# Another order of the same steps in a one-core kernel of attention, token mixing and a gated MLP

## The chip, the cores and the metric

The kernel runs on one core of one Trainium2 chip. The metric is the device time of one execution in microseconds (us). Lower is better.

## The reference

Three blocks follow each other, all in float32, for 2 batches of 768 tokens and 512 channels (8 heads of 64).

- Attention: each query sees the keys less than 16 places away, and 24 summaries of blocks of 32 tokens (the maximum of the block's keys, the mean of its values). One softmax runs over both.
- Token mixing: `theta = x @ w_theta`; `zr = x*cos(theta)`, `zi = x*sin(theta)`; `y = w_tok_r @ zr + w_tok_i @ zi` over the tokens; `u = x + y`; `x = u + max(u @ w_ch, 0)`.
- Gated MLP: `h = gelu(x @ w_in)`, split into u and v of 512 channels; v is normalised over its channels and mixed over the tokens with `w_sg`, plus `b_sg`; the result is `x + (u * v_s) @ w_out`.

## The kernel before

**Steps and plan.** The kernel defines some 1,670 named steps (`op`, line 272). Each is a small function that issues one to a few dozen instructions on one engine. The string `PLAN` (lines 49 to 258) lists them in the order in which they are issued. An entry reads `name.engine.places~step`: the engine is P (TensorE), V (VectorE), A (ScalarE), G (GpSimd) or S (SyncE, which issues the loads and stores); the places are a page of SBUF memory in units of 64 bytes, a PSUM bank or the number of a small buffer; `~step` makes the instruction wait for that step on another engine as well. `Steps.play` (line 283) goes through the plan and calls the functions; the framework adds the waits that the data and the reuse of memory ask for. Every engine works through its own steps strictly in the plan's order, so a step that waits holds up all later steps of its engine. The plan is text made beforehand by a search, with a model of durations that is not part of the kernel.

**Names.** The attention works on pairs of heads p = 0 to 7 (0 to 3 are batch 0) and on two halves of the queries. `k0`, `q0_1`, `vT0`, `v0_1` are loads. `ks`, `vs` are the block summaries of keys (VectorE) and values (GpSimd or VectorE); `vp`, `vm`, `vr` bring the value summaries beside the values. `S0_1` is the scores, `m`, `d`, `e` maximum, subtraction and exponential, `PT` and `Pt` the transposition and its copy to SBUF, `O0_1_0` and `O0_1_1` the product with the values for each head, `n` the division, `X` the transposed result, `xe`, `xh`, `xl` its copy and its split.

Matmuls run as three matmuls each on a high part and a remainder of both factors (`mm3`, lines 383 to 388), so each factor is split first (`...h` the high part, `...l` the remainder). The weights come as 64-bit floats: `wth2d` loads a piece, `wth2t` (ScalarE, line 518) and `wth2r` (VectorE, line 525) make float32 of it, `wth2h` and `wth2l` split it.

`th1_3` is a theta step: tile 1 of 12 token tiles, channel group 3. It needs `xl3_0` and `wth3l`. `kk`, `rr`, `ab`, `sc` reduce theta to one turn and take sine and cosine, `zm`, `zh`, `zl` multiply by x and split. `y0_1_2_0` is a token-mixing step of batch 0: token tile 1, channel quarter 2, with `w_tok_r`; it needs `zl1_1` and the split weights `wr1`, `wri1`. `uv` adds x. `ch`, `iv`, `iu` and `o` are the products with w_ch, the two halves of w_in and w_out. They use seven products of half-size blocks in place of eight, with sums of blocks (`u0_0+2`, `wv1+0`) prepared on VectorE and GpSimd. `mn`, `st`, `sq`, `rv`, `vo` normalise v, `vn` splits it, `sg` mixes it over the tokens, `ga` and `gm` gate, `g` prepares the result for w_out.

**Before the scores** TensorE runs 97 small matmuls (`fill`), and `idle0`, `idle1` are 6 and 1 matmuls whose results are not used; their numbers stand in `IDLE`.

**The order of the first 40 us.** These are the plan's steps of three engines in their own order.

SyncE before, up to `wth3d`: `k1 q1_0 k2 vT1 q2_0 k0 q0_0 vT0 q0_1 vT2 q1_1 v0_0 q2_1 wth0d v2_0 q3_0 v1_0 v0_1 vT3 k3 wth1d q3_1 v2_1 v3_1 v1_1 v3_0 wth2d wr0d k4 wth3d`

TensorE before, from `PT2_0` on: `PT2_0 O0_0_0 O1_0_0 O1_0_1 O0_0_1 PT0_1 PT2_1 X0_0 PT1_1 X1_0 vp3 S3_1 S3_0 O0_1_0 O0_1_1 O2_0_0 O2_0_1 O1_1_0 O1_1_1 O2_1_0 PT3_1 th0_0 X2_0 th2_0 X0_1 PT3_0 O2_1_1 O3_1_0 O3_1_1 O3_0_0 O3_0_1 th1_0 X1_1 th1_1 th2_1 X3_0 th0_1 X3_1 th5_0 th1_2 th0_2 th2_2 X2_1 th1_3 th0_3`

ScalarE before, from `e3_1` on: `e3_1 vr3_0 e3_0 Pt3_1 wth3t wth2t Pt3_0 xe2_0 xe0_1 xh2_0 xh0_1 wth2h xe1_1 wr0t wth3h xe3_0 wi0t`

Of the kernel before, what the change touches and what calls it, by code (L numbers as in the profile page):

```python
# [49 lines left out]
ones.V masks.G band.G k1.S.1536 warm.V.2716 fill.P.7 identb.V maskb.A ks1.V.5 q1_0.S.312 S1_0.P.6  # L50
m1_0.V.0 k2.S.2128 ks2.V.6 sums.G d1_0.V.195 vT1.S.416 q2_0.S.608 idle0.P.0 S2_0.P.4 k0.S.1055
ks0.V.2 m2_0.V.1 q0_0.S.1463 sets.G idle1.P.0 S0_0.P.0 e1_0.A d2_0.V.2691 vs1.G.4 vT0.S.240 vs0.G.0
vp1.P.6 PT1_0.P.2 m0_0.V.4 d0_0.V.723 q0_1.S.1512 S0_1.P.4 m0_1.V.1 vp0.P.7 vm1.A.0 e2_0.A vT2.S.96
q1_1.S.72 v0_0.S.2447 Pt1_0.A.2544 q2_1.S.455 d0_1.V.626 S2_1.P.1 m2_1.V.0 vm0.A.1 wth0d.S.2176
d2_1.V.3 e0_0.A wth0t.A.1 vs2.G.2 v2_0.S.783 PT0_0.P.6 S1_1.P.4 Pt0_0.A.240 q3_0.S.288 vp2.P.7
v1_0.S.1743 PT2_0.P.0 vr0_0.G m1_1.V.1 e0_1.A vr1_0.G vm2.A.2 v0_1.S.1103 e2_1.A O0_0_0.P.3
O1_0_0.P.2 wth0r.V.687 d1_1.V.1403 O1_0_1.P O0_0_1.P Pt2_0.A.479 n0_0.V.4.1632 n1_0.V.1
wth0h.A.1920 vT3.S.720 k3.S.192 e1_1.A ks3.V.4 PT0_1.P.0 Pt0_1.A.240 PT2_1.P.6 X0_0.P.3 xe0_0.A
# [14 lines left out]
xh3_1.G.864~wr1r kk2.A.687 S4_1.P.3 rr1.V.2496 vs4.V.1 xl1_1.G~wr1r v4_1.S.479 m4_0.V.2 kk0.A.1248
k6.S.528 wr0h.A.1088 xl2_1.G~wr1r xl3_1.G~wr1r th4_0.P.5 th4_1.P d4_0.V.315 v4_0.S.719 vp4.P.1
th3_0.P.2 th3_1.P th5_1.P th3_2.P wri1t.A.0 th3_3.P q6_0.S.288 m4_1.V.0 wri1r.V.1186 th4_2.P
q7_1.S.360 wri0r.V.639 wri0h.G.1024~wri0r rr0.V.2464 d4_1.V.578 rr2.V.1568 e4_0.A k5.S.2128
ab1_0.A.1600 PT4_0.P.3 vm4.A.1 ks6.V.1 sc1_0.A th4_3.P wi0h.G.960~wri0r ab0_0.A.1888 kk3.A.415
vr4_0.G~wri0r S6_0.P.0 sc0_0.A Pt4_0.A.312 vT5.S.2640 e4_1.A vT6.S.2256 O4_0_0.P.4 O4_0_1.P
wi0l.G~wri0r th5_2.P rr3.V.1536 vs5.V.2 m6_0.V.4 PT4_1.P.2 vr4_1.A wr0l.G~wri0r wri0l.G~wri0r
Pt4_1.A.671 n4_0.V.0.2592 th5_3.P X4_0.P.4 O4_1_0.P.2 kk4.A.736 O4_1_1.P zm0_0.G wr1h.A.2048  # L80
ks5.V.3 d6_0.V.419 S5_0.P.0 zh0_0.G.832 wi1d.S.1792 zl0_0.G zm1_0.G y0_0_0_0.P.6.3 v6_0.S.1351
vs6.V.4 rr4.V.2544 wri1h.A.1984 m5_0.V.0 vp5.P.5 vm5.V.2 xe4_0.A y0_0_0_1.P d5_0.V.1299 wi1t.A.2
q5_1.S.1223 S6_1.P.4 y0_0_1_0.P.0 wri1l.G v5_0.S.591 vp6.P.1 ab2_0.A.1888 zh1_0.A.896 wi1r.V.496
k7.S.288 y0_0_1_1.P sc2_0.A m6_1.V.1 d6_1.V.1747 S5_1.P.4 vT7.S.1400 n4_1.V.1.672 zl1_0.G~wi1r
wr1l.G~wi1r wi1h.G.768~wi1r y0_1_0_0.P vr5_0.A wi1l.G~wi1r vm6.A.1 e5_0.A PT5_0.P.1 ks7.V.0
y0_1_0_1.P m5_1.V.5 wr2d.S.1472 v5_1.S.1167 kk5.A.2112 zm2_0.G~wi1r zh2_0.G.832 d5_1.V.1843 zl2_0.G
v6_1.S.2399 v7_0.S.1247 e6_0.A rr5.V.2176 S7_1.P.4 y0_1_1_0.P Pt5_0.A.1296 wr2t.A.1 e5_1.A
PT5_1.P.1 vs7.V.2 wri2t.A.2 m7_1.V.4 d7_1.V.1798 ab5_0.A.1600 y0_1_1_1.P PT6_0.P.4 vr6_0.A vr5_1.G
O5_0_0.P.7 O5_0_1.P Pt5_1.A.2256 O5_1_0.P.2 O5_1_1.P wr2r.V.544 ab1_1.V.2208 Pt6_0.A.336
wr2h.G.896~wr2r S7_0.P.4 wri2r.V.512 n5_0.V.1 wri2h.A.128 wi2d.S.1856 n5_1.V.5 O6_0_0.P.1 O6_0_1.P  # L90
# [1105 lines left out]
```

## Time and profile before

| | |
|---|---|
| median of 3 runs | 377.17 us (375.05, 377.17, 377.32) |
| the profiled execution | 374.89 us, span 373.0 us |
| busy | PE 360.2 us (97%), DVE 293.0 (79%), ACT 216.6 (58%), POOL 162.8 (44%) |
| read from HBM, written | 36.86 MB, 3.15 MB |
| chain that ended last | PE 86%, DMA 7%, SPq 2%, ACT 2%, POOL 1%, DVE 1% |

The profile calls TensorE PE, VectorE DVE, ScalarE ACT, GpSimd POOL and SyncE SP. The span runs from the first to the last instruction. A row of a timeline names the start, the length, the engine, the line of the kernel, what is written and read, and in brackets the idle time before it with what ended it. `page4F` is a page of SBUF memory that many buffers use in turn, `banks` is PSUM. Lengths of neighbouring rows overlap a little, since an engine starts the next instruction before the last one's results are written.

### The profile page before, as it was taken

How to read it: one execution, taken by the hardware profiler on the slowest of the kernel's cores; microseconds unless marked ns; L12 is line 12 of the kernel's file. 1: busy time of each engine (PE TensorE's matmuls, PEld its weight loads, DVE VectorE, ACT ScalarE, POOL GpSimd, SP SyncE). 2: the span in 40 equal slices, each digit the busy share in tenths (PEclk: the TensorE clock that was granted, in tenths of full speed). 3: DMA queues.
4: the chain of work that ended last, by engine and by line, in shares of the span. 5: the costliest groups of instructions: out<-in, count | busy, mean ns of one | idle time of the engine just before them, and what ended most of it. 6: DMA issues, size and time to landing. Idle time of an engine off the chain costs nothing.

```text
span 373.0 us, 8181 instructions
## 1 busy us (share of the span) xinstructions
PE 360.2 (97%) x3236; PEld 333.2 (89%) x3236; DVE 293.0 (79%) x510; ACT 216.6 (58%) x419; POOL 162.8 (44%) x182
## 2 busy tenths in 40 slices
...
GB/s 247 320 305 377 292 176 225 192 194 188 154 81 37 269 14 140 84 58 45 56 0 99 2 1 2 84 3 201 41 0 2 0 3 56 57 2 0 23 84 232
DMA packets 16485, 40.52 MB, mean 109 GB/s; under 512 B 2240, under 2 KB 7872, under 8 KB 16448
## 3 DMA queue, kind: packets, MB, share of 16 engines
...
q8 instruction: 25, 0.41, 0.5%
q14 instruction: 12, 0.10, 0.1%
HBM read 36.86 MB, written 3.15 MB: 107 GB/s over the span
## 4 chain that ended last, share of the span: by engine, by line
PE 86%; DMA 7%; SPq 2%; ACT 2%; POOL 1%; DVE 1%; issue 1%; DVEq 0%; POOLq 0%
PE banks L386 27%; PE banks L387 26%; PE banks L388 26%; DMA page4F<-in_w_theta_dram 2%; PE banks L691 2%; DMA page2F<-in_vT_dram 2%; DMA page6F<-in_vW_dram 2%; DMA page4F<-in_vW_dram 2%; PE banks L675 1%; PE banks L712 1%; PE banks L644 1%; PE banks L651 1%; POOL page2F L584 1%; SPq L512 1%; PE banks L637 0%
## 5 line engine op out<-in xcount | busy, mean ns | idle before, releaser
L373 ACT ACTIVATE page3F<-banks 128x384 f32<-128x384 f32 (+2 forms) x19 | 8.9, 473 | 19.9 <-PE banks L388 17.0
L657 DVE TENSOR_REDUCE small<-banks 128x6 f32<-128x720 f32 x16 | 14.5, 904 | 3.9 <-PE banks L651 3.9
L373 ACT ACTIVATE page1F<-banks 128x384 f32<-128x384 f32 (+2 forms) x13 | 7.5, 580 | 10.6 <-PE banks L388 9.4
L805 DVE TENSOR_TENSOR xT<-banks,xT 128x256 f32<-128x256 f32 (+1 forms) x16 | 8.1, 551 | 4.3 <-PE banks L388 4.2
L1084 DVE SCALAR_TENSOR_TENSOR page13F<-banks,g_sb,page13F 128x384 f32<-128x384 f32 x8 | 4.8, 615 | 5.0 <-PE banks L388 5.0
L1111 POOL TENSOR_TENSOR page3F<-page3F,xT 128x384 f32<-128x384 f32 x3 | 3.1, 1025 | 11.9 <-ACT page3F L373 11.9
L373 ACT ACTIVATE page7F<-banks 128x256 f32<-128x256 f32 (+2 forms) x12 | 5.6, 485 | 4.0 <-PE banks L388 3.7
L373 ACT ACTIVATE xT<-banks 128x384 f32<-128x384 f32 x11 | 5.2, 486 | 3.2 <-PE banks L712 3.0
L387 PE MATMUL banks<-page9R,page5R 128*128 128x384 f32 (+2 forms) x22 | 7.1, 321 | 0.0
L388 PE MATMUL banks<-page9R,page5R 128*128 128x384 f32 (+2 forms) x22 | 7.1, 321 | 0.0
L386 PE MATMUL banks<-page9R,page5R 128*128 128x384 f32 (+2 forms) x22 | 7.0, 320 | 0.0
L876 POOL TENSOR_TENSOR page8F<-page13F,page12F 128x256 f32<-128x256 f32 x1 | 1.1, 1117 | 13.3 <-DVE page5R L381 13.3
L381 POOL TENSOR_TENSOR page0R<-xT,page0R 128x384 fp32r<-128x384 f32 x2 | 2.0, 1018 | 10.8 <-ACT page0R L373 6.5
L388 PE MATMUL banks<-page6R,page5R 128*128 128x384 f32 x20 | 6.7, 335 | 0.0
L387 PE MATMUL banks<-page6R,page5R 128*128 128x384 f32 x20 | 6.7, 334 | 0.0
L386 PE MATMUL banks<-page6R,page5R 128*128 128x384 f32 x20 | 6.7, 334 | 0.0
L1025 POOL TENSOR_SCALAR mv<-mv 128x1 f32<-128x1 f32 x7 | 1.8, 251 | 10.7 <-ACT page13F L999 4.9
L388 PE MATMUL banks<-page9R,page0R 128*128 128x384 f32 (+1 forms) x20 | 6.3, 314 | 0.0
L387 PE MATMUL banks<-page9R,page0R 128*128 128x384 f32 (+1 forms) x20 | 6.3, 313 | 0.0
L386 PE MATMUL banks<-page9R,page0R 128*128 128x384 f32 (+1 forms) x20 | 6.2, 312 | 0.0
L387 PE MATMUL banks<-page5R,page11R 128*128 128x512 f32 (+2 forms) x18 | 6.1, 340 | 0.0
L386 PE MATMUL banks<-page5R,page11R 128*128 128x512 f32 (+2 forms) x18 | 6.1, 338 | 0.0
...
## 6 DMA issues: line engine op xcount, KB each, us to landing
page13F<-in_w_in_dram SPq DMA_DIRECT2D x3, 511.8 KB, 3.8
...
page13F<-in_w_sgT_dram SPq DMA_DIRECT2D x3, 384.0 KB, 4.2
...
page9F<-in_w_iT_dram SPq DMA_DIRECT2D x2, 511.8 KB, 4.8
page11F<-in_w_iT_dram SPq DMA_DIRECT2D x2, 511.8 KB, 3.8
page11F<-in_w_ch_dram SPq DMA_DIRECT2D x2, 511.8 KB, 5.0
page1F<-in_w_in_dram SPq DMA_DIRECT2D x2, 511.8 KB, 3.9
```

The source lines that it names most:

```text
L373: ACT.activation(dst, src, AF.Copy)
L386: PE.matmul(ps, ah, bh, start=first, stop=False, skip_group_check=True)
L387: PE.matmul(ps, ah, bl, start=False, stop=False, skip_group_check=True)
L388: PE.matmul(ps, al, bh, start=False, stop=last, skip_group_check=True)
L512: nc.sync.dma_start(raw[:, c:c + n - 1], w[:, 1:])
L584: POOL.tensor_tensor(out=vv[:, :, :m], in0=vv[:, :, :m], in1=vv[:, :, m:2 * m], op=ALU.add)
L644: PE.matmul(s3(h)[sl(ab, 64), t, :WK], q[rr, sl(2 * t + ab, 64)], k[rr, FIRST[w]:FIRST[w] + WK], start=False, stop=True, skip_group_check= ...
L651: PE.matmul(s3(h)[sl(ab, 64), t, WK:], q[rr, sl(2 * t + ab, 64)], ks[rr, :], start=False, stop=True, skip_group_check=True)
L657: op(f"m{u}", "V", lambda e: DVE.tensor_reduce(out=m3(), in_=s4(), axis=AX.X, op=ALU.max, negate=True), after=[f"S{u}"], new=[(f"m{u}", "K ...
L691: PE.matmul(ps[64 * ab:64 * ab + 64, o:o + 65], sb[:WC, x:x + 64], v[:WC, c:c + 65], start=True, stop=True)
L805: DVE.tensor_tensor(out=dst, in0=ps, in1=dst, op=ALU.add)
L1084: DVE.scalar_tensor_tensor(out=T(gf)[:, s], in0=T(bk)[:, :384], scalar=g_sb[:, f:f + 1], in1=T("bsg")[:, s], op0=ALU.mult, op1=ALU.add)
```

## The change

Only `PLAN` and `IDLE` change. The plan was searched on with longer durations for the loads of value stretches (`v0_0` and the like), a shorter distance between uses of a PSUM block, and 8 constants in the early waits of its model. The new plan holds the same steps and one more, `idle2`, one matmul whose result is not used. The order and the places in memory differ nearly everywhere. 187 steps change their engine: 52 from GpSimd to VectorE and 44 back, 35 from ScalarE to VectorE and 28 back, 15 from GpSimd to ScalarE and 13 back. VectorE has 487 steps after 472, ScalarE 347 after 352, GpSimd 144 after 154. Of the 131 extra waits (`~`) 130 are left.

The new order of the same three engines:

SyncE: `k1 q1_0 k2 vT1 q2_0 k0 q0_0 vT0 q2_1 q0_1 vT2 q1_1 v1_0 v0_0 wth0d v0_1 k3 q3_1 vT3 wth1d v2_0 v1_1 q3_0 v3_0 v2_1 wth2d v3_1 wth3d wr1d vT5 wr0d k4 q4_1 wi0d q4_0 vT4 wri0d wri1d`

TensorE: `PT2_0 O0_0_0 O0_0_1 idle2 PT0_1 O1_0_0 O1_0_1 X0_0 PT2_1 PT1_1 X1_0 O0_1_0 S3_1 S3_0 O0_1_1 O1_1_0 O1_1_1 O2_0_0 O2_0_1 vp3 PT3_1 O2_1_0 O2_1_1 th0_0 X0_1 PT3_0 th2_0 X2_0 O3_1_0 O3_1_1 O3_0_0 O3_0_1 X1_1 th2_1 X2_1 th0_1 X3_0 th1_0 th1_1 th0_2 th1_2 th2_2 X3_1 th1_3 th0_3`

ScalarE: `e3_1 vm3 e3_0 Pt3_1 wth2t wth3t Pt3_0 xe2_0 xe0_1 xh2_0 wth2h wr0t wth3h wr1t xe3_0 xh3_0 xe2_1 wi0t`

The diff at `IDLE`, from 30 to 45 us, ahead of the second half of the token mixing (`y0_0_2_0`), and at the handover from `iv1` and `iu1` to `sg1`:

```diff
-IDLE = (6, 1,)
+IDLE = (6, 1, 1,)
...
-PT1_1.P.0 vs3.G.0~wth0r X1_0.P.5 vr0_1.G~wth0r wth1d.S.2624 wth1t.A.2 Pt2_1.A.2448 xe1_0.A
-q3_1.S.2692 vp3.P.4 S3_1.P.2 v2_1.S.406 Pt1_1.A.48 wth0l.V v3_1.S.1250 wth1r.V.1888 m3_1.V.1
-S3_0.P.6 O0_1_0.P.5 v1_1.S.527 v3_0.S.1054 wth2d.S.1186 O0_1_1.P vm3.A.1 vr2_0.G~wth1r O2_0_0.P.0
-O2_0_1.P d3_1.V.99 vr2_1.G~wth1r vr1_1.A m3_0.V.4 d3_0.V.3 wr0d.S.832 xh1_0.A.2208 O1_1_0.P.1
-O1_1_1.P k4.S.1584 e3_1.A O2_1_0.P.2 n2_0.V.0 n0_1.V.4.192 n1_1.V.1 vr3_0.A PT3_1.P.3
-xh0_0.G.2064~wth1r xl0_0.G~wth1r th0_0.P.6 e3_0.A Pt3_1.A.464 wth3d.S.896 vr3_1.G~wth1r wth3t.A.1
-X2_0.P.7 wth2t.A.0 th2_0.P.0 X0_1.P.3 PT3_0.P.4 Pt3_0.A.144 O2_1_1.P O3_1_0.P.1 xe2_0.A
-xl1_0.G~wth1r wth1h.G.2696~wth1r O3_1_1.P q4_0.S.1351 wth3r.V.512 O3_0_0.P.4 xe0_1.A q7_0.S.1448
-wri1d.S.1728 O3_0_1.P xh2_0.A.144 th1_0.P.5 wr1d.S.990 xh0_1.A.2016 X1_1.P.7 wth2r.V.1824 wth1l.V
-th1_1.P th2_1.P xl2_0.G~wth1l wri2d.S.2311 n2_1.V.4 n3_0.V.0 vT4.S.336 xl0_1.G~wth1l wi0d.S.2576
-q4_1.S.2664 wth2h.A.64 X3_0.P.3 n3_1.V.4 wth2l.V th0_1.P q5_0.S.391 xe1_1.A X3_1.P.1 th5_0.P.7
...
+vr0_1.G~wth0r e1_1.A wth0h.A.1920 vs3.G.5~wth0r wth1t.A.0 v1_1.S.406 PT1_1.P.0 q3_0.S.2736 X1_0.P.4
+O0_1_0.P.5 wth1r.V.687 Pt2_1.A.144 S3_1.P.2 S3_0.P.6 O0_1_1.P v3_0.S.1743 vr1_1.A Pt1_1.A.48
+O1_1_0.P.0 O1_1_1.P wth0l.V m3_1.V.1 xh0_0.G.2208~wth0l vr2_0.G~wth0l d3_1.V.315 O2_0_0.P.2
+O2_0_1.P wth1h.A.2696 xe1_0.A m3_0.V.4 d3_0.V.723 e3_1.A v2_1.S.783 vr2_1.G~wth0l wth2d.S.896
+xh1_0.G.2064~wth0l vp3.P.1 n0_1.V.1.192 vm3.A.1 PT3_1.P.3 xl0_0.G~wth0l v3_1.S.1103 O2_1_0.P.1
+O2_1_1.P n1_1.V.0 th0_0.P.6 e3_0.A Pt3_1.A.528 wth3d.S.2624 X0_1.P.7 n2_0.V.4 PT3_0.P.4
+vr3_0.G~wth0l th2_0.P.0 vr3_1.G~wth0l wr1d.S.990 n2_1.V.0 X2_0.P.3 vT5.S.2448 wth2t.A.2 wr0d.S.1792
+wth3t.A.1 Pt3_0.A.1055 O3_1_0.P.2 O3_1_1.P xl1_0.G xe2_0.A O3_0_0.P.5 O3_0_1.P k4.S.288 q4_1.S.1448
+wi0d.S.1186 xe0_1.A X1_1.P.3 xh2_0.A.144 wth2r.V.736 wth1l.V wth2h.A.64 th2_1.P wth3r.V.2496
+n3_0.V.1 X2_1.P.7 th0_1.P X3_0.P.4 q4_0.S.455 th1_0.P.5 vT4.S.2640 wri0d.S.1472 xl2_0.G~wth3r
+th1_1.P wth2l.V wr0t.A.1 wri1d.S.2576 wth3h.A.0 wr1t.A.2 wth3l.V xe3_0.A th0_2.P th1_2.P
+xh3_0.A.2064 xe2_1.A wr0r.V.1154 n3_1.V.2 th2_2.P X3_1.P.7 wi0t.A.1 ks4.V.1 xh0_1.G.2016~wr0r
+xe1_1.A xl3_0.G~wr0r wr1r.V.544 xh2_1.A.864 th1_3.P th0_3.P wi0r.V.576 S4_0.P.1 v4_0.S.719 S4_1.P.3
...
-zh1_1.A.1856 kk9.A.576 zh2_1.G.1920~wi5r wi3r.V.1152 y0_0_2_0.P.5.4 y0_0_2_1.P rr9.V.2112
-zl1_1.G~wi3r ab9_0.V.288 sc3_1.A zm3_1.G~wi3r y0_0_3_0.P.7 y0_0_3_1.P sc5_1.A zl2_1.V zh3_1.A.64
...
+wi3d.S.1600 wri4t.A.0 kk9.A.352 rr9.V.1664 zh1_1.G.2696~zl3_1 zl1_1.V zm5_1.V sc4_0.A ab8_1.A.1536
+wr5t.A.1 wr5r.V.576 sc4_1.A wi5h.A.1344 ab6_1.V.1696 zl3_0.V th10_3.P wri4r.V.1152 zh2_1.A.1856
+wi3t.A.1 wi3r.V.2112 wi3h.A.512 ab9_0.A.1184 zl2_1.G~wi3r wri3l.V wi3l.V wch0d.S.2240 sc6_0.A
+wri5t.A.1 wi4d.S.2319 zm4_0.V y0_0_2_0.P.5.4 y0_0_2_1.P y0_0_3_0.P.7 y0_0_3_1.P y0_1_2_0.P
...
-iu1_1C_0_1.P st1_2.A.4 iv1_012g.A iu1_1B_0_0.P.5 iu1_1A_3_1.P iu1_1B_0_1.P g0_0+3.G~g0_0+0
-iu1_022.V.2712 mn1_0.G st1_1.A.7 g0_0q1l.G st1_0.A.2 iu1_122.V.584 iu1_1C_1_0.P g0_0q2h.V.768 sq1.A
-g0_0q2l.G iu1_0C_1_0.P iu1_1C_1_1.P rv1.V vo1_1.A vo1_3.A vo1_0.V o0_1A_0_0.P.2 iu1_0B_0_0.P.7
-iu1_0C_1_1.P iu1_0B_0_1.P vo1_2.A vn1_0h.G.1664 iu1_111.V.608 vn1_2h.A.2368 iu1_112.V.632
-ut1_1_1g.A.264 vn1_0l.G vn1_3h.V.2304 iu1_012.V.360 vn1_1h.G.2432 o0_0B_0_0.P.4 iu1_011.V.240
-sg1_1_2_0.P.3 wout1d.S.1375 vo1_5.A o0_0A_0_0.P.7 sg1_1_3_0.P.5 vn1_1l.V g0_1q0h.V.2208
...
+st1_3.A.7 iv1_111.V.688 iv1_112.V iv1_112g.A mn1_2.G~g0_0+2 iu1_0C_0_0.P.6 st1_2.A.7 iu1_122.V.2712
+mn1_1.V iu1_0C_0_1.P iu1_1C_1_0.P iu1_1C_1_1.P mn1_0.V st1_1.A.4 st1_0.A.2 g0_0q1h.V.864
+g0_1q0l.G~g0_0+2 iu1_1B_0_0.P.7 iu1_022.V.584 iu1_1B_0_1.P g0_0q2h.V.768 iu1_112.V.608 sq1.A
+iu1_0B_0_0.P.2 iu1_0C_1_0.P ut1_1_1g.A.240 rv1.V iu1_0C_1_1.P iu1_0B_0_1.P g0_0q1l.G~g0_0+2 vo1_0.V
+g0_0q2l.G o0_0B_0_0.P.5 wout1d.S.1375 vo1_1.A vn1_0h.V.1664 vn1_0l.V sg1_1_2_0.P.3 iu1_012.V.2600
```

## Rows read from the trace of the kernel before

**Rows 1.** Stretches of the span: start:end, length, busy us of each engine, clock, DMA.

```profile
42.00:111.00 69.00, 68.69 (x899) 58.69 (x898) 57.31 (x100) 56.39 (x103) 41.95 (x43) 1.00 0.54 172
111.00:302.00 191.00, 190.97 (x1165) 179.62 (x1164) 150.18 (x262) 102.81 (x210) 67.71 (x62) 1.00 0.17 57
```

**Rows 2.** TensorE's waits: on whom, total us, times, longest.

```profile
PE banks L691 <- ACT page0F L373: 2.6, 1, 2.6
...
PE banks L386 <- POOL page12R L375: 1.5, 1, 1.5
```

**Rows 3.** TensorE's timeline, 23 to 39 us: start, length, line, tiles, idle time before.

```profile
23.84 0.49 PE L712 MATMUL banks<-ident,page8F 128*128 128x128 f32 x3
25.43 0.28 PE L601 MATMUL banks<-ident,small 128*24 128x128 f32 x1 [1.11 <-POOL small L586]
...
34.15 0.87 PE L691 MATMUL banks<-page6F,page2F 120*64 120x65 f32 x24
37.65 1.17 PE L691 MATMUL banks<-page5F,page0F 120*64 120x65 f32 x24 [2.63 <-ACT page0F L373]
```

**Rows 4.** ScalarE's timeline, 35 to 37 us: start, length, line, tiles.

```profile
35.55 0.77 ACT L518 ACTIVATE stage<-page4F 128x512 f16<-128x512 bf16 x1 [3.50 <-DMA page4F<-in_w_theta_dram]
36.20 0.75 ACT L518 ACTIVATE stage<-page6F 128x512 f16<-128x512 bf16 x1
36.82 0.78 ACT L373 ACTIVATE page0F<-banks 120x768 f32<-120x768 f32 x1
```

**Rows 5.** SyncE's timeline, issues from 26 to 28 us: start, length.

```profile
26.23 0.37 SPq L512 DMA_DIRECT2D page6F<-in_w_theta_dram  x1
26.70 0.38 SPq L512 DMA_DIRECT2D page4F<-in_w_rT_dram  x1
27.33 0.33 SPq L557 DMA_DIRECT2D page8F<-in_kT_dram  x1
27.84 0.33 SPq L512 DMA_DIRECT2D page4F<-in_w_theta_dram  x1
```

**Rows 6.** DMA issues of 26 to 29 us: count, KB, us to landing.

```profile
page6F<-in_w_theta_dram SPq DMA_DIRECT2D x1, 511.8 KB, 4.8
page4F<-in_w_rT_dram SPq DMA_DIRECT2D x1, 511.8 KB, 6.6
page4F<-in_w_theta_dram SPq DMA_DIRECT2D x1, 511.8 KB, 7.7
page8F<-in_kT_dram SPq DMA_DIRECT2D x1, 384.0 KB, 6.9
```

**Rows 7.** Single microseconds of the clock, columns as in the first group.

```profile
38.00:39.00 1.00, 1.00 (x21) 0.88 (x18) 0.93 (x4) 0.44 (x2) 0.00 (x0) 0.58 1.05 398
39.00:40.00 1.00, 1.00 (x3) 0.81 (x4) 0.93 (x5) 1.00 (x3) 0.48 (x1) 0.50 1.08 421
...
41.00:42.00 1.00, 1.00 (x5) 0.81 (x4) 1.00 (x1) 0.93 (x2) 0.51 (x1) 0.71 1.05 380
```

**Rows 8.** Chain that ended last, 312 to 316 us: start, length, what.

```profile
312.42 0.47 DVE page3F L1046
313.04 0.63 POOL page8R L375
313.74 1.28 POOL page8R L381
...
315.92 0.41 PE banks L386
```

**Rows 9.** TensorE's timeline, the first matmul of two theta steps in a row.

```profile
44.64 0.39 PE L386 MATMUL banks<-page0R 128*128 128x512 f32 x1
...
45.33 0.39 PE L386 MATMUL banks<-page0R 128*128 128x512 f32 x1
```

**Rows 10.** VectorE's timeline at 316 us, a subtraction and a cast.

```profile
316.16 0.68 DVE L381 TENSOR_TENSOR page12R<-page3F,page12R 128x512 fp32r<-128x512 f32 x1
316.76 0.35 DVE L378 CAST page11R<-page1F 128x384 fp32r<-128x384 f32 x1
```

374 lines of the change are left out of this document (185 added, 189 removed).

## The prediction

> **What bounds the kernel now.** I read the table by stretches first, then TensorE's waits, then the first 45 us engine by engine. From 42 to 302 us the tensor engine is the bound: 68.69 us busy of 69 and 190.97 of 191 [rows 1]. No order of the same matmuls can make that part shorter; it can only put waits into it. What an order can win lies in two places. One is the wait of 2.6 us on ScalarE at about 35 us, the other one of 1.5 us on GpSimd at 314 us [rows 2]. So the forecast is about the first 42 us, about the handover before the last gating stage, and about what new waits 270 full microseconds may get.
>
> **The wait at 35 us.** TensorE ends O3_1_1 at 35.02 (34.15 + 0.87) and starts O3_0_0 at 37.65 [rows 3]. O3_0_0 waits for vr3_0 and for Pt3_0, a ScalarE copy that began at 36.82. Ahead of Pt3_0 in ScalarE's order stand wth3t and wth2t, which began at 35.55 and 36.20 after 3.50 us of idling for a load of w_theta [rows 4]. Issue [rows 5] plus time to landing [rows 6] gives the landings: wth2 26.23 + 4.8 = 31.0, wr0 26.70 + 6.6 = 33.3, k4 27.33 + 6.9 = 34.2, wth3 27.84 + 7.7 = 35.5. The transfers land one after the other in the order of issue, so wr0 takes 2.3 us of the stream here, k4 0.9 and wth3 1.3. They stand back to back, so an order is priced by what stands ahead of the load that is waited for.
>
> **The change, part by part.** Up to O3_0_0, TensorE does the same steps in both plans; only idle2 is new. Up to wth3d, the loads are the same but for wr0d and k4, which now stand behind wth3d. With these two out of the way wth3 lands at 35.5 - 2.3 - 0.9 = 32.3. In the new ScalarE order wth2t and wth3t still stand ahead of Pt3_0, but wth2's load lands well before and only wth3t (0.65 to the next start) comes after 32.3. Then from Pt3_0's start to O3_0_0's are 37.65 - 36.82 = 0.83 us: 32.3 + 0.65 + 0.83 = 33.8 from this side.
>
> TensorE itself needs longer. In the old order vp3 waited 1.11 us at 25.43 for GpSimd's sums of vT3 [rows 3]; the new order puts vp3 behind O2_0_1, some 4 us of work later, and the sums come from the same place in the load order, so that wait goes. What is late next is q3_0, now issued behind v2_0 and v1_1: S3_0 needs it. The trace doesn't show this wait. Its bounds are 0 and the 1.11 us of the wait that it replaces; I take 0.3, as S3_1, O0_1_0 and idle2 now stand in front of it and give it nearly 2 us more. idle2 is one matmul of filler, 0 to 0.4 us; I take 0.4, since TensorE has no hole there. So TensorE is ready for O3_0_0 at 35.02 - 1.11 + 0.3 + 0.4 = 34.6, after ScalarE's 33.8. O3_0_0 moves from 37.65 to 34.6: **minus 3.05 us** (bounds 1.9 and 3.9: the whole 1.11 and more at S3_0, or no wait and idle2 free).
>
> **The clock.** After the 2.63 us hole the granted clock was 0.58, 0.50, 0.50 and 0.71 in the four microseconds from 38 to 42 [rows 7], that is the lower level (1.2 GHz) for (0.42 + 0.50 + 0.50 + 0.29) / 0.5 = 3.4 us, all of them with matmuls waiting in line. That is 1.7 us of full-speed work lost. The 1.11 us wait at 25.43 was not followed by a lower clock. The waits that I expect in the new start are shorter than that one, so **minus 1.7 us**.
>
> **Behind O3.** wr0d is now third behind wth3d (wr1d, vT5, wr0d). At the prices of wth3, k4 and wr0 it lands at 32.3 + 1.3 + 0.9 + 2.3 = 36.8. In ScalarE's order wr0t stands ahead of wth3h, wr1t, xe3_0 and xh3_0, and th1_3 and th0_3 need the last. Five starts at 0.65 or less make it 40.1 at most, GpSimd's xl3_0 (1.28 at most, the price of a larger tile [rows 8]) 41.4. TensorE comes to th1_3 behind two halves of O3 (0.87), four X (0.25 to 0.49 each [rows 3]) and seven theta steps of 0.69 [rows 9]: 34.6 + 0.9 + 1.0 to 2.0 + 4.8 = 41.3 to 42.3. A wait of 0 to 1 us; I take **plus 0.3**. vT4 and wri1d now take wth3d's place in memory and hold SyncE's queue until wth3r has read it, but five loads are ahead of them by then, so the stream doesn't run dry; nothing for that. The next stage starts earlier by what was won, and its loads (k4, q4) stand right behind wr0d.
>
> **The handover at 314 us.** In the old order the last steps of the chain are vo1_0 on VectorE, then vn1_0's high part and remainder on GpSimd (0.63 + 1.28); TensorE starts the first step that uses them at 315.92, 3.5 us after vo1_0's start [rows 8]. The new order has both on VectorE: a cast costs it 0.35 for 384 columns, the subtraction 0.68 for 512 [rows 10], so about 0.47 + 0.4 + 0.68 = 1.6 us instead of 3.5. The work on TensorE that covers the chain is 15 steps in both orders. Against that, two sums and the splits of g0_0 (VectorE) stand ahead of rv1, and two last adds of iv1 stand later, together up to 1 us. Bounds: 0 and the whole wait of 1.5; I take **minus 1.0**.
>
> **The rest.** VectorE gets 15 steps more, GpSimd 10 and ScalarE 5 fewer; what hides them is TensorE's packed stretch. A new order has waits of its own: behind 42 us the old one has two, of 0.3 (69 - 68.69) and of 1.5 us. I allow one of their mean size, **plus 0.9**, bounds 0 and 3. The last two steps, their sums and stores are the same.
>
> **Sum.** -3.05 - 1.7 + 0.3 - 1.0 + 0.9 = -4.55 us. The profiled execution took 374.89 us (span 373.0), so the same execution would take 370.3. The median shown is 377.17, 2.3 above it; one of the three runs, 375.05, is like the profile, two are not. What sets them apart the trace can't show. If it is events of the start, the change takes some of it away; I carry 1.5 of the 2.3. **Predicted: 371.8 us**, its own range 368.8 to 373.8.
>
> **Rivals.**
> A, the change doesn't do what it says at the start: wth2t and wth3t still stand ahead of Pt3_0, and if the loads of v and vT that now come early take the time that wr0 and k4 gave up, the hole of over 2 us and its half clock stay. For it: ScalarE's order is unchanged there. Against it: the same loads are ahead of wth3d but two. It gives back 3.05 + 1.7: 376.5.
>
> B, the lower clock comes without the long hole. The row shows none after 1.11 us. The Trainium skill (TensorE: Matmul & The Clock Gate, Part 1: The HAM clock gate) says that the monitor behind the clock is not tied to the kernel's start, so that runs of the same kernel spend different lengths at the lower clock; no run here shows that. By that rule a wait at S3_0 or th1_3 may bring the half clock in one run and not in another. As a mechanism here: one such stretch costs 1.7 us, 371.8 + 1.7 = 373.5.
>
> C, slower: VectorE becomes the bound between O3_0_0 and the second half of the token mixing (y0_0_2_0). In the old order 108 VectorE instructions stand there, in the new 120. At 57.31 us for 100 [rows 1] that is 68.8 us of work; TensorE's steps in between last about as long, 69 us. zl1_1, the 110th (63.0 us), is needed by y0_1_2_0, four steps of about 1 us behind y0_0_2_0, so at 73. VectorE may thus idle 10 us on the way, and in the old order it idled 69 - 57.3 = 11.7. If the new one idles as much, TensorE waits 1.7 us; from 13.7 us of idling on, with the half clock behind the hole, the kernel is slower than before (371.8 + 3.7 + 1.7 = 377.2); at 15 us it is 378.5. For it: the counts. Against it: VectorE idled in the old order because it had nothing due, and all other halves of z and of the weights have more room.
>
> **How the numbers follow.** Forecast 0.60, A 0.12, B 0.15, C 0.10, something else 0.03. The range reaches from the forecast's low end, 368.8, over B to A, 376.8; left out are C, the upper part of A and the forecast's tail, under 0.2. A measurement of this kernel tells about 1% from no change, that is 373.4 and 380.9. Faster: 0.60 x 0.9 and 0.4 of B, 0.60. Slower: a third of C and the rest, 0.05. Same: 0.35.
>
> **What would show it.** Right: O3_0_0 at 34 to 35 us with no wait over 1 us before it, clock 1.00 from 25 us on, th1_3 at 41 to 42, a wait of at most 0.5 us before the first sg1 step, and 42 to 300 us full. Wrong: a TensorE wait on ScalarE or a load of over 2 us in the first 45 us with the clock at 0.5 after it (A or B); waits of y0_1_2_0 or a later y0 step on VectorE's remainders (C); or waits of the handover's kind spread over ch0, iv0 or sg0, which I have allowed only 0.9 us.

## The result, and the profile after

The changed kernel takes 370.26 us (median of 6 runs, 369.80 to 371.75), the kernel before in the same comparison 375.40 (6 runs, 374.23 to 377.32). The ratio is 0.9858 with a 95% interval of 0.9824 to 0.9892, so it is 1.4% faster, clear of the noise. One run of experiment 5 below, over 1.5% above the fastest of its kernel, is left out of that experiment's median. The profiled execution took 369.80 us with a span of 368.1; before it was 374.89 and 373.0. Line numbers of the new kernel are one lower than those of the old one (L385 for L386 and so on).

The table by stretches comes first, as in [rows 1] and [rows 7] (start:end, length, busy time of TensorE, its weight loads, VectorE, ScalarE and GpSimd, granted clock, DMA share, GB/s):

```profile
28.00:29.00 1.00, 1.00 (x42) 1.00 (x40) 0.96 (x2) 1.00 (x3) 0.50 (x1) 1.00 1.05 297
29.00:30.00 1.00, 1.00 (x30) 0.93 (x26) 0.97 (x3) 0.60 (x1) 0.94 (x2) 1.00 1.00 304
...
33.00:34.00 1.00, 1.00 (x8) 0.83 (x7) 0.95 (x2) 0.97 (x2) 0.39 (x1) 1.00 1.03 417
...
38.00:39.00 1.00, 1.00 (x8) 0.87 (x7) 1.00 (x2) 0.94 (x2) 0.00 (x0) 1.00 1.04 405
39.00:40.00 1.00, 1.00 (x6) 0.82 (x5) 0.93 (x5) 0.32 (x1) 0.51 (x1) 1.00 1.03 381
...
42.00:105.00 63.00, 63.00 (x872) 54.09 (x871) 55.62 (x96) 52.88 (x92) 38.00 (x39) 1.00 0.58 182
105.00:300.00 195.00, 195.00 (x1195) 183.55 (x1194) 154.78 (x274) 105.31 (x222) 72.97 (x65) 1.00 0.17 58
```

From 38 to 40 us the clock is 1.00 where it was 0.58 and 0.50 [rows 7]. From 42 to 300 us TensorE is full to the hundredth, as it was nearly before [rows 1]. So hardly a wait can have been won there. Most was won ahead of 42 us and a little at the handover; another 0.7 us, most of it in no wait that the profile shows, was won between 42 and 144 us (the part on the prediction comes back to it). TensorE's waits, in the columns of [rows 2]:

```profile
PE banks L643 <- DMA page3F<-in_qT_dram: 1.1, 1, 1.1
PE banks L643 <- DMA page14F<-in_qT_dram: 1.0, 1, 1.0
...
PE banks L385 <- DVE page3F L1065: 0.5, 1, 0.5
PE banks L385 <- DVE page8R L377: 0.4, 1, 0.4
```

The 2.6 us on ScalarE are gone. The 1.5 us on GpSimd have become 0.4 and 0.5 on VectorE. New is 1.0 us on q3_0's load (page14F). The 1.1 us on page3F lie at 8.73 us, ahead of the part that was changed on purpose; that wait differs between executions of one and the same order (0.46 us in experiment 4, 1.61 in experiment 5). TensorE's timeline shows where they lie; it answers to [rows 3] and, from 308 us on, to [rows 8]:

```profile
25.46 0.32 PE L636 MATMUL banks<-maskb,identb 64*64 64x288 bf16 x4
26.79 0.73 PE L643 MATMUL banks<-page3F,page14F 64*64 64x96 f32 x24 [1.01 <-DMA page14F<-in_qT_dram]
...
29.66 0.28 PE L600 MATMUL banks<-ident,small 128*24 128x128 f32 x1
...
34.26 0.92 PE L690 MATMUL banks<-page5F,page2F 120*64 120x65 f32 x24
35.01 0.87 PE L690 MATMUL banks<-page9F,page5F 120*64 120x65 f32 x24
...
308.93 0.45 PE L385 MATMUL banks<-page9R,page8R 128*128 128x384 f32 x1 [0.36 <-DVE page8R L377]
...
313.17 0.44 PE L385 MATMUL banks<-page11R,page0R 128*128 128x384 f32 x1 [0.46 <-DVE page3F L1065]
```

O3_0_0 starts at 35.01 right behind O3_1_1, and vp3 (29.66) no longer waits. S3_0 starts at 25.46 and waits inside for q3_0. On ScalarE, as in [rows 4], the conversion of wth2 now waits for no load, and that of wth3 waits 0.65 us for its own:

```profile
31.62 0.77 ACT L517 ACTIVATE stage<-page4F 128x512 f16<-128x512 bf16 x1
33.03 0.80 ACT L517 ACTIVATE stage<-page13F 128x512 f16<-128x512 bf16 x1 [0.65 <-DMA page13F<-in_w_theta_dram]
33.68 0.79 ACT L372 ACTIVATE page5F<-banks 120x768 f32<-120x768 f32 x1
```

The issues of wth3 and wr0 (columns of [rows 5]) and their time to landing ([rows 6]):

```profile
26.76 0.51 SPq L511 DMA_DIRECT2D page13F<-in_w_theta_dram  x1
...
28.34 0.59 SPq L511 DMA_DIRECT2D page9F<-in_w_rT_dram  x1
```

```profile
page13F<-in_w_theta_dram SPq DMA_DIRECT2D x1, 511.8 KB, 6.2
...
page9F<-in_w_rT_dram SPq DMA_DIRECT2D x1, 511.8 KB, 8.2
```

wth3 lands at 26.76 + 6.2 = 33.0 (35.5 before), wr0 at 36.5 (33.3 before). Last, VectorE at the handover, in place of the GpSimd rows of [rows 8]:

```profile
308.44 0.43 DVE L377 CAST page8R<-page3F 128x512 fp32r<-128x512 f32 x1
308.91 0.69 DVE L380 TENSOR_TENSOR page8R<-page3F,page8R 128x512 fp32r<-128x512 f32 x1
...
309.98 2.21 DVE L1045 TENSOR_SCALAR page10F<-page10F,mv,rs 128x512 f32<-128x512 f32 x2
...
312.58 0.54 DVE L1065 TENSOR_TENSOR page3F<-banks,page3F 128x384 f32<-128x384 f32 x1
```

The high part is ready at 308.87, and TensorE starts on it at 308.93. But VectorE then does vo1_2 and vo1_3 (2.21 us) ahead of the last sum of iu1 (312.58), for which o0_1A_0_0 waits the 0.46 us shown above.

One more row of the old chain belongs beside [rows 8], between vn1_0's remainder and TensorE's start. It is vn1_1's high part, a third step on GpSimd, and the old timeline puts the end of TensorE's wait on it and not on vn1_0:

```profile
315.03 0.77 POOL page12R L375
```

```profile
315.92 0.41 PE L386 MATMUL banks<-page6R,page8R 128*128 128x384 f32 x1 [1.46 <-POOL page12R L375]
```

### The profile page after: what moved, and what is told of

It reads as the page before. It is cut to its first block, busy times and chain, and to the rows that moved or that the text cites. A ratio compares the mean times of both kernels' runs of the same rounds, so it can differ in the third digit from the quotient of the medians.

```text
span 368.1 us, 8188 instructions
## 1 busy us (share of the span) xinstructions
PE 358.0 (97%) x3237; PEld 330.9 (90%) x3237; DVE 300.1 (82%) x525; ACT 215.2 (58%) x414; POOL 156.7 (43%) x172
## 4 chain that ended last, share of the span: by engine, by line
PE 89%; DMA 4%; DVE 2%; ACT 2%; SPq 1%; POOL 1%; issue 0%; DVEq 0%
PE banks L385 27%; PE banks L386 26%; PE banks L387 26%; PE banks L690 3%; PE banks L674 2%; DMA page1F<-in_vT_dram 2%; PE banks L643 2%; DMA page14F<-in_qT_dram 2%; PE banks L711 1%; ACT banks L1026 1%; PE banks L650 1%; POOL page1F L583 1%; PE banks L636 1%; DVE page10F L1045 1%; SPq L568 1%
## 5 line engine op out<-in xcount | busy, mean ns | idle before, releaser
L372 ACT ACTIVATE page3F<-banks 128x384 f32<-128x384 f32 (+1 forms) x14 | 6.5, 468 | 19.6 <-PE banks L387 12.0
L372 ACT ACTIVATE page1F<-banks 128x384 f32<-128x384 f32 (+1 forms) x13 | 7.7, 590 | 11.0 <-PE banks L387 9.6
L385 PE MATMUL banks<-page6R,page12R 128*128 128x384 f32 x24 | 8.0, 334 | 0.0
L386 PE MATMUL banks<-page6R,page12R 128*128 128x384 f32 x24 | 8.0, 334 | 0.0
L387 PE MATMUL banks<-page6R,page12R 128*128 128x384 f32 x24 | 8.0, 334 | 0.0
L380 POOL TENSOR_TENSOR page4R<-xT,page4R 128x384 fp32r<-128x384 f32 x3 | 3.1, 1021 | 11.4 <-DVE page6R L380 7.6
L1083 DVE SCALAR_TENSOR_TENSOR page1F<-banks,g_sb,page13F 128x384 f32<-128x384 f32 x10 | 6.0, 612 | 1.7 <-PE banks L387 1.6
L385 PE MATMUL banks<-page9R,page5R 128*128 128x384 f32 (+2 forms) x22 | 7.3, 333 | 0.0
L386 PE MATMUL banks<-page9R,page5R 128*128 128x384 f32 (+2 forms) x22 | 7.3, 331 | 0.0
L583 POOL TENSOR_TENSOR page8F<-page8F 128x384 f32<-128x384 f32 (+3 forms) x8 | 4.5, 564 | 6.0 <-DMA page8F<-in_vT_dram 5.6
L517 ACT ACTIVATE stage<-page11F 128x512 f16<-128x512 bf16 x6 | 4.7, 785 | 4.1 <-DMA page11F<-in_w_ch_dram 3.6
L380 POOL TENSOR_TENSOR page4R<-page1F,page4R 128x512 fp32r<-128x512 f32 (+1 forms) x3 | 4.4, 1480 | 5.7 <-ACT page4R L372 3.2
L385 PE MATMUL banks<-page6R,page2R 128*128 128x384 f32 x20 | 6.7, 335 | 0.0
L386 PE MATMUL banks<-page6R,page2R 128*128 128x384 f32 x20 | 6.7, 335 | 0.0
L387 PE MATMUL banks<-page6R,page2R 128*128 128x384 f32 x20 | 6.7, 334 | 0.0
L875 POOL TENSOR_TENSOR page8F<-page12F,page3F 128x256 f32<-128x256 f32 x1 | 5.3, 5275 | 2.7 <-DVE page4R L380 2.7
```

Of the source, the lines that this page charges most:

```text
L372: ACT.activation(dst, src, AF.Copy)
L380: EN[e].tensor_tensor(out=lo, in0=src, in1=hi.bitcast(F32), op=ALU.subtract)
L385: PE.matmul(ps, ah, bh, start=first, stop=False, skip_group_check=True)
L386: PE.matmul(ps, ah, bl, start=False, stop=False, skip_group_check=True)
L387: PE.matmul(ps, al, bh, start=False, stop=last, skip_group_check=True)
L583: POOL.tensor_tensor(out=vv[:, :, :m], in0=vv[:, :, :m], in1=vv[:, :, m:2 * m], op=ALU.add)
```

## The experiments

The theory: the gain is the order of two loads (wr0 and k4 behind wth3), by the hole that it closes and by the half clock behind that hole; the handover adds a few tenths. The rival ideas were ScalarE's order, TensorE's own new order at the start, and the handover. Times below are medians. The kernel before, measured beside them, took 375.53 (22 runs) with the first four experiments, 375.61 (17 runs) with the next four, 376.39 (11) and 375.87 (16) with the last two. In the diffs, " ... " within a line leaves out entries of the plan.

**1. The old kernel with the two loads moved, and nothing else.**

```diff
-O2_0_1.P d3_1.V.99 vr2_1.G~wth1r vr1_1.A m3_0.V.4 d3_0.V.3 wr0d.S.832 xh1_0.A.2208 O1_1_0.P.1
-O1_1_1.P k4.S.1584 e3_1.A O2_1_0.P.2 n2_0.V.0 n0_1.V.4.192 n1_1.V.1 vr3_0.A PT3_1.P.3
...
+xh0_0.G.2064~wth1r ... Pt3_1.A.464 wth3d.S.896 wr0d.S.832 k4.S.1584 vr3_1.G~wth1r wth3t.A.1
```

> The kernel before with two loads moved: wr0d and k4 are issued behind wth3d, nothing else. Theory (these two loads stood ahead of wth3d, ScalarE's conversion of wth3 held up Pt3_0, and the hole brought the lower clock): wth3d lands 3.2 us earlier, at about 32.3, O3_0_0 starts at about 35.0 without a hole, the clock stays at 1.00 from 38 to 42 us, and the time falls by 2.6 + 1.7 = 4.3 us against the kernel before (3.4 to 4.8). Rival 1 (the gain of the new plan comes from its order as a whole, VectorE's steps and the middle): 0 to 1.5 us faster. Rival 2 (the hole only moves, since wr0 is now late for what needs it): O3_0_0 early, but a wait of 1 to 3 us by 50 us, 1 to 3 us faster.

It took 372.02 us (370.53 to 374.53), ratio 0.9884 [0.9841, 0.9926]. TensorE's timeline:

```profile
25.77 0.28 PE L601 MATMUL banks<-ident,small 128*24 128x128 f32 x1 [1.40 <-POOL small L586]
...
35.18 0.87 PE L691 MATMUL banks<-page5F,page0F 120*64 120x65 f32 x24
```

No hole is left before O3_0_0, the clock is 1.00 throughout, and the last matmul ends 4.22 us earlier than in the profile of before (364.99 for 369.21); 4.3 was expected. The wait of vp3 (1.40) and the one at the handover (1.44) stay. Two loads moved in an otherwise old plan give 3.5 of the 5.1 us by the medians, and 4.2 of 5.3 us at the last matmul of the profiled executions. Three of the six runs here have a lower mean clock, which holds the median up (the table at the end of this section).

**2. The new kernel with the two loads put back ahead of wth3.**

```diff
-O2_1_1.P n1_1.V.0 th0_0.P.6 e3_0.A Pt3_1.A.528 wth3d.S.2624 X0_1.P.7 n2_0.V.4 PT3_0.P.4
+O2_1_1.P n1_1.V.0 th0_0.P.6 e3_0.A Pt3_1.A.528 wr0d.S.1792 k4.S.288 wth3d.S.2624 X0_1.P.7 n2_0.V.4 PT3_0.P.4
```

> The new kernel with wr0d and k4 moved back ahead of wth3d, nothing else. Theory: wth3d lands at 33.0 + 3.2 = 36.2, Pt3_0 starts at 36.9, O3_0_0 at 37.7 behind a hole of about 2.6 us, and the clock is at the lower level for about 3.4 us after it: 2.7 + 1.7 = 4.4 us slower than the new kernel, 374.7, that is 1 us or less faster than the kernel before. Rival 1 (order as a whole): 0 to 1.5 us slower than the new kernel. Rival 2 (the clock stays up, since TensorE was busier before the hole): 2.7 slower, 373.

It took 372.27 us (371.38 to 374.32), 2.0 more than the changed kernel (1.6 in the profiled executions), where the theory said 4.4. wth3 landed at 35.0, and the hole came back at half its old size. The timeline and a microsecond behind it:

```profile
36.54 0.92 PE L690 MATMUL banks<-page9F,page5F 120*64 120x65 f32 x24 [1.33 <-ACT page5F L372]
```

```profile
38.00:39.00 1.00, 1.00 (x7) 0.85 (x6) 1.00 (x2) 1.00 (x3) 0.77 (x1) 1.00 1.01 391
```

The clock stayed at 1.00. So the sign is as expected and the size is not: the load came 1.2 us earlier than the 36.2 expected, which took as much from the hole, and the shorter hole had no half clock behind it. SyncE's timeline of wr0, k4 and wth3, and SyncE's wait in front of k4, show that the edit did more than swap places:

```profile
27.10 0.52 SPq L511 DMA_DIRECT2D page9F<-in_w_rT_dram  x1
30.35 0.35 SPq L556 DMA_DIRECT2D page1F<-in_kT_dram  x1
30.75 0.43 SPq L511 DMA_DIRECT2D page13F<-in_w_theta_dram  x1
```

```profile
SPq L556 <- PE banks L674: 2.7, 1, 2.7
```

k4 waited 2.7 us until TensorE had read what lay in its place in memory, and held wth3's issue up. With 5.7, 3.4 and 4.3 us to landing, wr0 came at 32.8, about where wth3 had come (33.0), k4 at 33.8 and wth3 at 35.0. The two loads thus cost 2.0 us here, not the 3.2 read off the old order.

**3. The old kernel with Pt3_0 ahead of the two w_theta conversions on ScalarE.**

```diff
-X2_0.P.7 wth2t.A.0 th2_0.P.0 X0_1.P.3 PT3_0.P.4 Pt3_0.A.144 O2_1_1.P O3_1_0.P.1 xe2_0.A
+X2_0.P.7 th2_0.P.0 X0_1.P.3 PT3_0.P.4 Pt3_0.A.144 wth3t.A.1 wth2t.A.0 O2_1_1.P O3_1_0.P.1 xe2_0.A
```

> The kernel before with one change in ScalarE's order: Pt3_0 stands ahead of wth3t and wth2t; the loads are as they were and wth3d lands at 35.5. Theory (Pt3_0 was held up only by standing behind the conversions): O3_0_0 at about 35.0, no hole, clock at 1.00, 3.5 to 4.3 us faster than the kernel before; th1_2 and th2_2, which need wth2, are 5 us behind O3_0_0 and wait little. Rival (the loads of w_theta bound the start, whoever stands in front): O3_0_0 early, but TensorE waits for wth2 or wth3 by 45 us, and the gain is under 2 us.

It took 374.68 us (372.57 to 376.29), ratio 0.9957 [0.9928, 0.9985]. O3_0_0 starts at 34.67 with no hole, earlier than in any other kernel here, and yet little is won (0.9 us by the medians; 2.5 us at the last matmul of the profiled execution, one of only three runs of twelve without a lower mean clock):

```profile
37.36 0.55 PE L712 MATMUL banks<-ident,page1F 128*128 128x128 f32 x3 [0.92 <-ACT xT L373]
...
40.23 0.52 PE L712 MATMUL banks<-ident,page8F 128*128 128x128 f32 x3 [0.44 <-DVE small L699]
```

The conversions have to be done anyway, and the late load now holds them and what stands behind them (the first wait above is for a copy behind them on ScalarE). To step around the late load moved over half of the wait here; the earlier load of experiment 1 removed it.

**4 and 5. The new kernel with wth3's conversion done 3 times, then 5 times, to hold ScalarE up ahead of Pt3_0.**

```diff
-            ACT.activation(T(nm + "s", F16).rearrange("p (n t) -> p n t", t=2)[:, :, 1],
-                           raw[:, :, 2], AF.Copy)
+            for _ in range(3 if nm == "wth3" else 1):
+                ACT.activation(T(nm + "s", F16).rearrange("p (n t) -> p n t", t=2)[:, :, 1],
+                               raw[:, :, 2], AF.Copy)
```

> The new kernel with two more copies of wth3's conversion on ScalarE (the same result three times), 2 x 0.65 us. ScalarE's side of O3_0_0 had 33.68 + 0.83 = 34.5 against 35.0 on TensorE's, so O3_0_0 starts at 35.8 behind a hole of 0.8 us. Theory (TensorE bounds the rest, a hole of this size does not bring the lower clock): 0.8 us slower than the new kernel, up to 1.2 if xl3_0 becomes late for th1_3. Rival (any hole here brings the lower clock): 2.5 us slower with the clock near 0.5 for 3 us. Rival 2 (there is slack behind O3_0_0): no change.

> The new kernel with four more copies of wth3's conversion on ScalarE, 4 x 0.65 us. Pt3_0 starts at 36.3, O3_0_0 at 37.1 behind a hole of 2.1 us. Theory (a hole near the old one's 2.6 us brings the lower clock): 2.1 + 1.7 = 3.8 us slower than the new kernel. Rival (the lower clock of the kernel before had another cause than the hole): 2.1 us slower, clock at 1.00 throughout.

With 3 it took 372.37 us (371.40 to 375.66), 2.1 more than the changed kernel, where 0.8 to 1.2 was expected. In the profiled execution wth3's load was issued at 27.90 (26.76 in the changed kernel) and came at 34.4, so the hole was 1.61 us where 0.8 was expected, and the clock stayed at 1.00. With 5 it took 374.41 (372.21 to 376.60, 11 runs), 4.2 more than the changed kernel, where 3.8 was expected. Its timeline (line 690 has become 691) and two microseconds behind the hole:

```profile
38.53 1.57 PE L691 MATMUL banks<-page9F,page5F 120*64 120x65 f32 x24 [2.45 <-ACT page5F L372]
```

```profile
39.00:40.00 1.00, 1.00 (x22) 0.91 (x18) 0.00 (x0) 1.00 (x3) 0.27 (x1) 0.50 0.57 180
40.00:41.00 1.00, 1.00 (x6) 0.97 (x5) 0.71 (x3) 1.00 (x3) 0.74 (x1) 0.50 0.89 307
```

In this execution a hole of 2.45 us brings back both the wait and the half clock of the old kernel. (It has a second half clock near 11 us, which the edit doesn't touch.) The half clock does not come in every run: three of the eleven have a mean clock of 1.000 and a median of 373.01, 2.8 above the changed kernel, which is about the hole alone. From the other side than experiment 1 this shows what the old start cost: the hole, and in most runs the half clock.

**6. The new kernel with vn1_0's two parts on GpSimd again.**

```diff
-g0_0q2l.G o0_0B_0_0.P.5 wout1d.S.1375 vo1_1.A vn1_0h.V.1664 vn1_0l.V sg1_1_2_0.P.3 iu1_012.V.2600
+g0_0q2l.G o0_0B_0_0.P.5 wout1d.S.1375 vo1_1.A vn1_0h.G.1664 vn1_0l.G sg1_1_2_0.P.3 iu1_012.V.2600
```

> The new kernel with both parts of vn1_0's split on GpSimd, as in the kernel before. GpSimd takes 0.62 + 1.28 us for them where VectorE took 0.43 + 0.69, and it is busy with g0_0q2l until 307.9. Theory (the handover hangs on this split): the first sg1 step starts 0.8 to 1.5 us later, the wait in front of it grows from 0.36 to between 1.2 and 1.9, and the time grows by as much, less what the wait of 0.46 us at o0_1A_0_0 gives back: 0.6 to 1.5 us. Rival (the split is hidden, the wait is set by ScalarE's and VectorE's steps before it): under 0.3 us.

It took 371.11 us (370.09 to 372.88), 0.85 more than the changed kernel. But the edit is at 310 us, and the profiled execution reaches y1_0_0_0, the first step of the second batch's token mixing, already 1.59 us later (145.24 and 143.65). So the part behind it is read, from y1_0_0_0 to the last matmul, one execution of each: 220.40 us, against 220.26 in the changed kernel. The handover itself:

```profile
310.74 0.45 PE L385 MATMUL banks<-page9R,page8R 128*128 128x384 f32 x1 [0.61 <-POOL page8R L374]
...
312.15 0.45 PE L387 MATMUL banks<-page9R,page8R 128*128 128x384 f32 x1 [0.78 <-POOL page8R L380]
```

TensorE waits longer here (0.61 + 0.78), but VectorE gets to vo1_2 and the sums of iu1 earlier, and the 0.46 us at o0_1A_0_0 are gone. What VectorE saves at the first step it mostly pays back at the next: 0.14 us is left. That the move from GpSimd to VectorE wins the handover has fallen. The rival has the size right (under 0.3 us) but not the reason, since the split is not hidden.

**7. The new kernel without idle2.** (The filler step is taken out of the plan.)

```diff
-IDLE = (6, 1, 1,)
+IDLE = (6, 1,)
...
-k3.S.720 O0_0_0.P.6 q3_1.S.360 O0_0_1.P e2_1.A vT3.S.1536 n0_0.V.1.1632 vm2.A.1 idle2.P.0 PT0_1.P.0
+k3.S.720 O0_0_0.P.6 q3_1.S.360 O0_0_1.P e2_1.A vT3.S.1536 n0_0.V.1.1632 vm2.A.1 PT0_1.P.0
```

> The new kernel without idle2, its one new step. Theory (one matmul of filler in a stretch where TensorE has no hole, but waits 1.0 us for q3_0 a few us later): the wait at S3_0 grows by what is saved, no change, under 0.2 us either way. Rival (it holds TensorE up): 0.4 us faster. Rival 2 (it keeps the clock up): the clock falls at 27 us and the time grows by over 1 us.

371.01 us (369.64 to 372.73), O3_0_0 at 35.38, S3_0's wait 1.28 us in place of 1.01: no difference in time that these runs can tell.

**8. The new kernel with q3_0 loaded earlier and Pt3_0 ahead of the conversions.**

```diff
-O1_0_0.P.2 ... xe0_0.V wth1d.S.832 v2_0.S.479 PT2_1.P.6 ks3.V.0
-vr0_1.G~wth0r ... v1_1.S.406 PT1_1.P.0 q3_0.S.2736 X1_0.P.4
+O1_0_0.P.2 ... xe0_0.V wth1d.S.832 q3_0.S.2736 v2_0.S.479 PT2_1.P.6 ks3.V.0
+vr0_1.G~wth0r ... v1_1.S.406 PT1_1.P.0 X1_0.P.4
...
-vr3_0.G~wth0l ... vT5.S.2448 wth2t.A.2 wr0d.S.1792
-wth3t.A.1 Pt3_0.A.1055 O3_1_0.P.2 ...
+vr3_0.G~wth0l ... vT5.S.2448 Pt3_0.A.1055 wth2t.A.2 wr0d.S.1792
+wth3t.A.1 O3_1_0.P.2 ...
```

> The new kernel with two moves: q3_0 is issued ahead of v2_0 and v1_1, and Pt3_0 stands ahead of wth2t and wth3t on ScalarE. Theory (from 15 us on TensorE is the bound, and S3_0's wait of 1.0 us for q3_0 is the only hole up to 300 us): q3_0 lands 2 us earlier, S3_0's wait goes, O3_0_0 starts at about 34.0, and the time falls by 0.7 to 1.0 us. Rival (the loads bound the start, the wait moves to v1_1's and v2_0's users, O1_1_0 or O2_0_0, or to th1_3, which had 0.6 us of room): under 0.4 us.

It took 369.77 us (369.72 to 371.56), ratio 0.9853 [0.9819, 0.9887]. Its profile has no wait in S3_0. Its profiled execution took 371.46, and shows why. TensorE's waits near 10 us and the clock just behind them:

```profile
8.95 0.73 PE L643 MATMUL banks<-page7F,page3F 64*64 64x96 f32 x24 [1.50 <-DMA page3F<-in_qT_dram]
...
11.09 1.24 PE L643 MATMUL banks<-page6F,page7F 64*64 64x96 f32 x24 [0.54 <-DMA page7F<-in_qT_dram]
```

```profile
11.00:12.00 1.00, 0.92 (x24) 0.94 (x28) 0.97 (x2) 0.00 (x0) 0.13 (x1) 0.56 1.06 398
12.00:13.00 1.00, 1.00 (x34) 0.95 (x29) 0.49 (x1) 0.00 (x0) 0.99 (x1) 0.50 0.82 224
```

That is a half clock in the first loads' waits, of the same size as that of [rows 7], in a kernel four of whose six runs are 1.7 us faster. By the medians the two moves win 0.5 us over the changed kernel, between the theory's 0.7 to 1.0 and the rival's 0.4.

**9. Experiment 8 with two sums of iu1 put ahead of vo1_2 on VectorE.**

```diff
-ut1_1_0g.A.264 sg1_1_1_0.P.4 vo1_4.A vo1_2.V vo1_3.V vn1_1h.G.384~vn1_0l vn1_2h.A.2432
-sg1_1_0_0.P.0 sg1_0_2_0.P.6 iu1_111.V.2688 iu1_011.V.664 vn1_3h.V.512 vn1_1l.G~vn1_0l sg1_0_0_0.P.1
+ut1_1_0g.A.264 sg1_1_1_0.P.4 vo1_4.A iu1_111.V.2688 iu1_011.V.664 vo1_2.V vo1_3.V vn1_1h.G.384~vn1_0l vn1_2h.A.2432
+sg1_1_0_0.P.0 sg1_0_2_0.P.6 vn1_3h.V.512 vn1_1l.G~vn1_0l sg1_0_0_0.P.1
```

> Theory: two waits of the kernel after are left, 1.0 us in S3_0 for q3_0 and 0.46 us at o0_1A_0_0 behind iu1_011, which VectorE does behind vo1_2 and vo1_3 (2.2 us). Here q3_0 is loaded before v2_0 and v1_1, Pt3_0 goes ahead of two w_theta conversions, and iu1_111 and iu1_011 go ahead of vo1_2. The wait at o0_1A_0_0 goes, and from y1_0_0_0 to the last matmul it is 219.8 us in place of 220.26; the median is 0.3 to 0.5 us below that of the kernel after by the start (as in the earlier run with that part alone) and 0.46 by the sums: 369.4. Rival: vn1_2 and vn1_3 come 1.1 us later and a later sg1 step waits as long as o0_1A_0_0 did: 220.2 us from y1_0_0_0, and a median of 369.8.

It took 370.21 us (369.64 to 371.41), ratio 0.9828 [0.9803, 0.9853]. The wait at o0_1A_0_0 is gone. A later step waits 0.23 us in its place:

```profile
317.76 0.44 PE L387 MATMUL banks<-page9R,page2R 128*128 128x384 f32 x1 [0.23 <-POOL page2R L380]
```

From y1_0_0_0 to the last matmul it is 220.01 us: 0.25 of the 0.46 is won. Both medians expected (369.4 and 369.8) were missed; the profiled execution, the slowest of the six, waits 0.87 us ahead of th2_0 at 34.97 and starts O3_0_0 only at 36.93. In 8 and 9 the intervals overlap with that of the changed kernel, so neither is shown to beat it. Both beat the old kernel.

**10. The old kernel with three moves: the loads of 1, ScalarE's order of 3, and vp3 with its copy vm3 behind O2_0_1.**

```diff
-q3_1.S.2692 vp3.P.4 S3_1.P.2 v2_1.S.406 Pt1_1.A.48 wth0l.V v3_1.S.1250 wth1r.V.1888 m3_1.V.1
-S3_0.P.6 O0_1_0.P.5 v1_1.S.527 v3_0.S.1054 wth2d.S.1186 O0_1_1.P vm3.A.1 vr2_0.G~wth1r O2_0_0.P.0
+q3_1.S.2692 S3_1.P.2 v2_1.S.406 Pt1_1.A.48 wth0l.V v3_1.S.1250 wth1r.V.1888 m3_1.V.1
+S3_0.P.6 O0_1_0.P.5 v1_1.S.527 v3_0.S.1054 wth2d.S.1186 O0_1_1.P vr2_0.G~wth1r O2_0_0.P.0
+O2_0_1.P vp3.P.4 vm3.A.1 d3_1.V.99 vr2_1.G~wth1r vr1_1.A ...
```

> The kernel before with three moves at the start: wr0d and k4 behind wth3d (as in the first experiment), Pt3_0 ahead of wth3t and wth2t on ScalarE (as in the third), and vp3 with its copy vm3 behind O2_0_1. Theory: with the loads in order, ScalarE and TensorE share the rest of the start's bound, so the three together give what neither of the last two gave alone: vp3's wait of 1.1 to 1.4 us goes, O3_0_0 starts at 33.9 to 34.3 (35.18 with the loads alone), no wait at the X steps over 0.3 us, and the end is 0.9 to 1.2 us ahead of the kernel with the loads alone: a median of 370.9 to 371.1 where that one had 372.0. Rival: the start is bound by the landing of the loads (w_theta and those behind it), so a wait comes back behind O3_0_0, at the X or theta steps: 371.8 to 372.2.

It took 375.80 us (372.58 to 377.89), ratio 0.9996 [0.9959, 1.0032]: the whole gain of the loads is lost, and both expectations missed. TensorE, then ScalarE:

```profile
26.39 0.72 PE L644 MATMUL banks<-page1F,page14F 64*64 64x96 f32 x24 [1.42 <-DMA page14F<-in_qT_dram]
...
31.42 0.92 PE L691 MATMUL banks<-page2F,page0F 120*64 120x65 f32 x24 [1.29 <-ACT page2F L373]
...
37.31 0.87 PE L691 MATMUL banks<-page5F,page0F 120*64 120x65 f32 x24
```

```profile
30.23 0.27 ACT L373 ACTIVATE sums<-banks 24x128 f32<-24x128 f32 x1 [2.09 <-PE banks L601]
30.52 0.85 ACT L373 ACTIVATE page2F<-sums 24x774 f32<-24x774 f32 x1
```

vp3's wait had covered two things. S3_1 comes to its load of q3_1 sooner and waits 1.42 us; but the load was also late in this execution, at 26.3 (20.14 + 6.2) where it landed at 25.0 to 25.5 in the three other profiles with this order of loads up to there (before, experiments 1 and 3), so at most 0.5 us of this wait belongs to the move. And vm3, now late, stops ScalarE for 2.09 us ahead of vr1_1, for which O1_1_0 waits 1.29. O3_0_0 starts at 37.31, with no hole before it and at full clock. The changed kernel also puts vp3 behind O2_0_1, but has q3_1 loaded by then and vr1_1 ahead of vm3. A step moved alone is not the step moved in a plan that makes room for it.

**The clock over all runs.** Every run has a mean granted clock. The profiles give a rough key. Ahead of the last matmul there is no half clock in the changed kernel's (0.998), one in that of before [rows 7] and in that of experiment 8 (0.995 each), two in that of experiment 5 (0.990, one near 11 us and one behind the hole). Some microseconds behind the last matmul the clock goes to the lower level in every profile, which takes up to 0.003 off the mean. Runs of a kernel, counted by their mean clock, with their median in us:

| kernel | 0.997 and over | 0.993 to 0.996 | 0.988 to 0.992 | 0.987 and under |
| --- | --- | --- | --- | --- |
| before, 66 runs | 2: 374.30 | 34: 375.41 | 24: 376.89 | 6: 377.53 |
| after, 6 runs | 5: 370.25 | 1: 371.75 | 0 | 0 |
| experiment 1, 6 runs | 3: 370.66 | 2: 372.02 | 1: 374.53 | 0 |
| experiment 5, 11 runs | 3: 373.01 | 4: 374.23 | 4: 375.85 | 0 |
| experiment 8, 6 runs | 3: 369.72 | 3: 371.46 | 0 | 0 |
| experiment 9, 6 runs | 5: 370.25 | 1: 369.83 | 0 | 0 |
| experiment 10, 12 runs | 4: 373.95 | 5: 376.88 | 3: 377.39 | 0 |

The mean clock is not all that sets the runs apart. Runs of one column still spread (374.11 to 377.33 in the second of the kernel before, 374.51 to 377.84 in that of experiment 10), and one run at 0.993 each is among the fast ones in experiments 8 (369.78) and 9 (369.83).

## Why the prediction was right, and where it was off

The forecast held: 371.8 us was predicted and 370.26 measured, faster, inside the range. By its own steps, in profiled executions:

- **O3_0_0 to 34.6 (minus 3.05).** It came to 35.01, minus 2.64. (The far bound, minus 3.9, was a slip: with no wait and idle2 free TensorE is ready at 33.9, minus 3.75.) The wait of S3_0, taken as 0.3, was 1.01, near the upper bound of 1.11: q3_0 landed at 26.75. Counting O3_1_1's end as the start of the next step gave back some of it, since the next starts 0.17 us before that end (34.26 + 0.92 against 35.01). wth3 landed at 33.0, not 32.3, although it was issued as early as in experiment 1 (26.76 and 26.81), where it did land at 32.3. The new order has the value load v3_1 between wth2 and wth3, and in the stretch of 28 to 30 us the stream brought 297 and 304 GB/s, and 417 at 33; that v3_1 is the reason is likely, but no run shows it. It did not matter, as TensorE, not ScalarE, was last, as forecast.
- **The clock (minus 1.7).** Right. The same work up to th1_3 is done 4.31 us earlier, 1.67 more than at O3_0_0.
- **th1_3 (plus 0.3).** No wait. wr0 landed at 36.5 (36.8 predicted), th1_3 started at 41.95 (41.3 to 42.3 predicted).
- **42 us to y1_0_0_0.** The prediction had it that no order can make this part shorter. Yet another 0.7 us was won there (4.31 to 5.02). Of it, 0.3 is the idle time that the old stretch had [rows 1]; for 0.4 I have no place. A stretch in which TensorE is busy to the hundredth can still be longer or shorter for the same steps.
- **The handover (minus 1.0) and new waits (plus 0.9).** At sg1_1_2_0 the wait fell by 1.1 (1.46 to 0.36), as forecast; 0.46 came back at o0_1A_0_0, one of the new waits allowed for. Net the end moved from 5.02 to 5.30 us, 0.28, against 0.1 in the sum. The reason given, VectorE's shorter split, does shorten that wait (0.36 for 0.61 + 0.78 in experiment 6), but is worth only 0.14 us of time. The chain it was priced on was also read short: of the 3.5 us up to TensorE's start, 0.9 lie behind vn1_0, with vn1_1's high part.
- **The sum.** 370.3 for the profiled execution, 369.80 measured. That it is so near is in part luck: the start of O3_0_0 fell 0.4 us short, and the wait at th1_3 that did not come (0.3), the stretch behind 42 us (0.7) and the handover (0.2) made up for it. Behind the last matmul 0.2 us was lost.
- **The 1.5 us carried from the median: this is the term that was off.** The median of before stood 2.3 us above its profile in the three runs shown, and 0.5 in the six of the comparison; after stands 0.46 above its own. What sets the runs apart goes in part with the mean clock: from column to column of the table 1.1, 1.5 and 0.6 us in the old kernel and 1.5 in the new one. By that key the old kernel had at least one half clock in 64 of 66 runs, the new one in 1 of 6. The carry should have been about half a microsecond. Of the 1.5 us between forecast and measurement, 1.0 is this term and 0.5 the sum.

**Rivals.** A did not come: O3_0_0 has no hole, and experiment 2 shows what the two loads, with the wait for k4's place, give back in the new order, 2.0 us. C did not come: zl1_1 began at 105.99, y0_1_2_0 at 110.05 without a wait, though VectorE is busy 55.62 of 63 us. B, the lower clock without the long hole, is seen in the profile of experiment 8, though near 11 us and not at S3_0 or th1_3, and likely in one of six runs of the changed kernel (371.75, mean clock 0.995; no profile of it was kept). The price that was put on it, 1.7 us, fits both (1.7 and 1.5). The Trainium skill (TensorE: Matmul & The Clock Gate, Part 1: The HAM clock gate) says that the clock's monitor does not restart with the kernel, so that equal kernels see it differently; the runs agree as far as they go, with mean clocks of 0.982 to 0.999 for the one old kernel, but why these differ no run shows.

What the experiments do not settle is the rest of the start, the 0.8 us by which the changed kernel reaches y1_0_0_0 ahead of experiment 1 (143.65 and 144.43). The waits of vp3 (1.40) and S3_0 (1.01) do not explain it: O3_0_0 starts only 0.17 us apart (35.01 and 35.18), and the other 0.6 comes behind it, where neither trace shows a wait on TensorE. That is the same stretch for whose 0.4 us against the old kernel I have no place. Experiment 10, which was to test the start, brought its own waits.
